# An attention and feed-forward kernel on one core: the turned keys of a unit are written later and read back earlier

## The chip, the cores and the metric

The kernel runs on one core of a Trainium2 chip. The metric is the device time of one execution in microseconds (us). Before the change it is 505.19 us, the median of 3 runs (504.56 to 507.04).

## The reference, cut to what matters

A gated linear attention over 4 batches, 8 heads, 768 steps and a head size of 48 feeds a feed-forward layer with a squared ReLU:

```python
f = 1.0 / (1.0 + np.exp(-f_logit))
for t in range(S):
    state = f[:, :, t, :, None] * state + np.einsum('bhd,bhe->bhde', k[:, :, t], v[:, :, t])
    y[:, :, t] = np.einsum('bhd,bhde->bhe', q[:, :, t], state)
x = y.transpose(0, 2, 1, 3).reshape(B * S, H * D)      # 3072 x 384
h = x @ w_in                                           # 384 -> 2048
r = np.maximum(h, 0.0)
out = (r * r) @ w_out                                  # 2048 -> 384
```

## The kernel before, in words

**Blocks and pieces.** Time is cut into 6 blocks of 128 steps; a block has 512 columns (4 batches by 128 steps). The feed-forward layer of a block goes through 16 pieces of 128 hidden features. For each piece `Moe.run` (L280) issues: `up` (L227, 9 matmuls into a PSUM bank `ph`, two banks taken in turn), `square` (L253, three ACT passes, the last of which writes `gh`), `rest` (L264, one DVE pass that writes `gl` and frees the bank) and `down` (L270, 9 matmuls into the three banks `po`) for the piece two before. Every product is made of three matmuls of high and low parts. The last `down` of a block is owed: it is issued in the first piece of the next block (`before()`, L306), and `finish` (L335) behind it copies the three `po` banks, two on ACT and one on DVE, into tiles `ob` and stores each with a DMA from the SP queue. The tiles `ob` share the buffers of `gh` and `gl` (three of each, L194 and L343), so a later `gh` can only be written when the store that read its buffer has landed. Block 0's second half is an exception: its results are added into tiles `part` of their own.

**Numbering.** After a prologue the pieces run in the order block 1 (pieces 0 to 15), the second half of block 0 (16 to 23), block 2 (24 to 39), block 3 (40 to 55), block 4 (56 to 71), block 5 (72 to 87). Pieces 24, 40, 56 and 72 are first pieces, with the end of the block before in them; so is 16.

**Units.** The attention of a block is 4 units of two heads. Units 8 to 23 (blocks 2 to 5) are woven into the pieces as hooks. The last unit of each block works on keys and queries that the first three hand to it. A unit has a slot, a piece in which its sums are made (`SLOTS`, L65: 12, 14, 18, 20, 22, 28, 31, 34, 37, 44, ...), and for the first three of a block the stages before it stand in `STAGE_AT` (L62), as a number of pieces ahead of the slot and a place in the piece: 0 ahead of `up`, 0.5 behind `square`, 0.7 behind `rest`, 1 at the end of the piece. The stages:
- "L" (L432) and "v" (L441): loads of gates, keys and queries, and of values.
- "GK" (L445, L448) and "Q" (L461): a sigmoid on ACT, then a scan and a product each for keys and queries on DVE, with two small steps on POOL between.
- "t" (`squares`, L514): DVE transposes the keys in squares of 32 by 32 (L517), and four DMAs of SP (L523) write them to `steps` in DRAM, so that time lies along the rows.
- "b" (`back`, L528): one DMA of SP (L530) loads the turned keys from `steps` into `kn`. `kn` has a single buffer.
- The slot itself, at 0.7: "Y" (L594) the outputs of the unit before, "D" (`add`, L545, matmuls L550 of `kn` with the values) and "S" (L556) the sums of this unit, "H" and "X" (L626, L640), which take the outputs of the unit before out of PSUM, then "M", "C" and the moves "m" (L472) and "l" (L532) for the block's last unit.

**What sets the order.** Every engine and the SP queue run their instructions in the order in which the hooks issue them; nothing is reordered. A DMA of SP whose data isn't ready holds all that stand behind it on SP. In one place of one piece, hooks run in the order in which they were registered: the slots and stages unit by unit. Unit 8 has its slot in piece 12 and its "t" in piece 8; unit 9 has its slot in piece 14 and its "t" in piece 10.

Of the kernel before, what the change touches and what calls it, by code (L numbers as in the profile page):

```python
# [58 lines left out]

STAGE_AT = ((-8, 1, "L"), (-5, 0, "v"), (-5, 1, "GK"), (-4, 0.5, "Q"), (-4, 0.7, "t"), (-2, 1, "b"))  # L62
LAST_AT = ((-5, 0, "v"),)

SLOTS = (12, 14, 18, 20, 22, 28, 31, 34, 37, 44, 47, 50, 53, 60, 63, 66, 69)  # L65
# [297 lines left out]
def fast_path(ctx, tc, moe, ident, low, fkqT, vN, w, w4, out):  # L363
# [37 lines left out]
    def weights_load(f, i, mark=False):  # L401
        raw = moe.words(f, i)
        if mark:

            V.memset(raw[0:1, 0:1], 0)
        nc.sync.dma_start(raw, w[f, i].bitcast(I16)[:, 1:])
# [293 lines left out]
    def step(t):  # L700

        nm = t.rstrip("0123456789")
        n = int(t[len(nm) :])  # L710
        if nm == "busy":
            if 0 not in moe.ph:
                moe.bank(0)
            for _ in range(n):
                nc.tensor.matmul(moe.ph[0], lhsT=one.broadcast_to([P, P]), rhs=one.broadcast_to([P, NT]), start=True, stop=True)
        elif nm in ("i", "o"):
            weights_load(n, "io".index(nm))
        elif nm == "j":
            nc.sync.dma_start(moe.fourth_words(), w4.bitcast(I16)[:, 1:])
        elif nm in "enaw":  # L720
            if nm == "e":
                decoding["fourth"] = moe.decode(moe.row4, moe.fourth_parts)
            next(decoding["fourth"])
        elif nm in "AIcJBOdP":
            i = "AIcJBOdP".index(nm) // 4
            if nm in "AB":
                decoding[n, i] = moe.decode(moe.row[n, i], lambda: moe.parts(n, i))
            next(decoding[n, i])
        elif nm in ("ua", "ub", "uc"):
            moe.up_part(n, "abc".index(nm[1]))  # L730
        elif nm == "U" and n < SPLIT:
            moe.up_fourth(n)
        elif nm == "U":
            moe.up(n)
        elif nm == "R":
            moe.square(n)
        elif nm == "E":
            moe.rest(n)
        elif nm == "W":
            moe.down(n)  # L740
        else:
            unit(n).stage(nm)
            if t == "G0":
                for head in moe.head[1:]:
                    nc.scalar.copy(out=head, in_=moe.head[0])
            elif t in ("K1", "K2"):
                for x in xs[0][:2] if n == 1 else xs[0][2:]:
                    G.memset(x[C + 32 :].bitcast(F32), 0.0)
# [7 lines left out]
    with tc.manual_schedule(engines={ET.PE, ET.SP, ET.DVE, ET.Activation, ET.Pool}):  # L756
        with tc.tile_pool(name="ps_p", bufs=2, space=bass.MemoryType.PSUM) as ps_p:
            for t in FIRST.split():
                step(t)
        moe.psum(ctx, "ps_h1", "ps_o")  # L760

        moe.sums_of()
        for t in SECOND.split():
            step(t)
        part = []
        owed = moe.ending(lambda po: part.extend(moe.keep(po)))
        whole = half[0] + half[1]
        order = [(1, whole), (0, half[1])] + [(blk, whole) for blk in range(2, NBLK)]
        hooks = [{} for _ in order]

        def hook(k, n, at, do):
            while n >= len(order[k][1]):
                k, n = k + 1, n - len(order[k][1])
            hooks[k].setdefault((max(n, 0), at), []).append(do)

        def third():
            early.close()
            moe.inputs(ctx)
            xs[2] = moe.new_x(2, 2)

        halves = [(f, i) for f in half[1] for i in range(2)]
        steps = {}

        def advance(h):
            if h not in steps:
                steps[h] = moe.decode(moe.row[halves[h]], lambda: moe.parts(*halves[h]))
            next(steps[h], None)

        for n in range(1, NF - 1):
            few = range(3 * (n - 1) // 2, min(3 * n // 2, len(halves)))
            for h in few:
                if n < AHEAD:
                    weights_load(*halves[h])
                else:
                    hook(0, n - AHEAD, 0.5, lambda h=h: weights_load(*halves[h], mark=True))

            def before(few=few):
                for h, last in zip(few, (None, *few)):  # L800
                    for m in (h, h, last):
                        if m is not None:
                            advance(m)

            def after(few=few[:-1]):
                for h in few:
                    advance(h)

            def last(few=few):
                for h in few[-1:]:  # L810
                    advance(h)
                    advance(h)


            for place, do in zip((0, 0.5, 0.7) if n > 1 else (0.7, 0.7, 0.7), (before, after, last)):
                hook(0, n, place, do)
        hook(0, 12, 0, third)
        later = [Unit(n, xs, (ps_a,)) for n in range(2 * HP, NBLK * HP)]
        for un, last, at in zip((*later, None), (None, *later), SLOTS):
            if un:  # L820
                for n, place, stage in STAGE_AT if un.own else LAST_AT:
                    hook(0, at + n, place, lambda un=un, stage=stage: un.stage(stage))

            def slot(un=un, last=last):
                for who, stage in (last, "Y"), (un, "DS"), (last, "HX"), (un, "rMC"), (un, "ml" * bool(un and un.own)):
                    if who:
                        who.stage(stage)
                if last and not last.own:
                    last.stage("hg")

            hook(0, at, 0.7, slot)
            if un:
                hook(0, at + 1, 0, lambda un=un: un.stage("s"))

        for n in range(2 * NF):
            hook(2 + n // NF, n % NF + SIZES_AT, 1, lambda n=n: moe.sizes(n // 2, n % 2))
        general = []
        found = verdict(nc, moe, low, ident, ps_a)
        for n in range(2):
            hook(len(order) - 2, VERDICT_AT + n, 1, lambda: general.append(next(found)))  # L840
        hook(
            len(order) - 1, VERDICT_AT, 1,
            lambda: general.append(nc.values_load(general[1][0:1, 0:1], min_val=0, max_val=1)),
        )
        for k, (blk, fs) in enumerate(order):
            if blk > 1 and blk + 1 < NBLK:
                xs[blk + 1] = moe.new_x(blk + 1, (0, 1, 2)[blk - 2])
            moe.begin(blk, xs[blk], fs)
            if blk == NBLK - 1:

                moe.third_bank = ps_a
                obs = moe.third_of("ob_last")
                moe.run(hooks[k], obs, owed)
                moe.third_bank = None
            else:
                moe.run(hooks[k], None, owed)
                owed = moe.ending(
                    lambda po, blk=blk: moe.finish(
                        lambda e: out[blk, e * P : (e + 1) * P], None if blk else part, po, blk
                    )  # L860
                )
# [3 lines left out]
def verdict(nc, moe, low, ident, pool):  # L865

    flag = moe.const.tile([1, 1], I32, name="flag")
    good = moe.const.tile([P, 2], F32, name="good")
    nc.vector.tensor_reduce(
        out=good[:, 0:1], in_=low.rearrange("p u n -> p (u n)"), axis=mybir.AxisListType.X, op=ALU.min  # L870
    )
    nc.vector.tensor_scalar(out=moe.sums, in0=moe.sums, scalar1=LARGE, scalar2=None, op0=ALU.is_lt)
    nc.vector.tensor_reduce(out=good[:, 1:2], in_=moe.sums, axis=mybir.AxisListType.X, op=ALU.min)
    nc.vector.tensor_tensor(out=good[:, 0:1], in0=good[:, 0:1], in1=good[:, 1:2], op=ALU.min)
    yield
    pl = pool.tile([1, P], F32, tag="pk", name="pl")
    nc.tensor.transpose(out=pl, in_=good[:, 0:1], identity=ident)
    least = moe.const.tile([1, 1], F32, name="least")
    nc.vector.tensor_reduce(out=least, in_=pl, axis=mybir.AxisListType.X, op=ALU.min)
    nc.vector.tensor_scalar(out=least, in0=least, scalar1=LOWEST, scalar2=None, op0=ALU.is_le)  # L880
    nc.vector.tensor_copy(out=flag, in_=least)
    yield flag
# [185 lines left out]
```

## Time and profile before

| | before |
|---|---|
| median of 3 runs | 505.19 us (504.56 to 507.04) |
| the profiled execution, its own time | 503.3 us |
| its span, first to last instruction | 501.5 us |
| TensorE (PE) busy | 474.3 us, 95% of the span |
| PE weight loads (PEld) | 380.2 us, 76% |
| DVE / ACT / POOL busy | 249.1 / 284.2 / 29.7 us |
| mean granted TensorE clock | 0.987 |

A page of the profile gives busy times by engine, the chain of work that ended last (followed back from the last instruction), the costliest groups of instructions and the DMA issues. The trace behind it can be asked for a timeline of single instructions, for who waited for whom, and for busy times and clock in a stretch. An instruction that waits is not busy; its idle time stands in brackets, with what ended it.

### The profile page before, as it was taken

What the parts mean: (1) busy time and instruction counts of PE and PEld (TensorE: products, weight loads), DVE (VectorE), ACT (ScalarE), POOL (GpSimd) and SP (SyncE); (2) the same over time, 40 slices, a digit from 0 to 9 for tenths busy, and PEclk for the clock granted to TensorE, in tenths of its full rate; (3) what the DMA queues carried; (4) which work ended last, traced back from release to release, by engine and by line L of the source; (5) the groups of instructions that cost most, each with busy time, mean ns of one, the idle gap of its engine ahead of it and who ended that gap; (6) DMA issues with size and microseconds to landing.
All of it is one profiled execution on the core that took longest, in us unless ns stands there. A gap on an engine that the chain in (4) does not pass through costs nothing.

```text
span 501.5 us, 11437 instructions
## 1 busy us (share of the span) xinstructions
PE 474.3 (95%) x4767; PEld 380.2 (76%) x4767; DVE 249.1 (50%) x456; ACT 284.2 (57%) x591; POOL 29.7 (6%) x66
## 2 busy tenths in 40 slices
PE   3889999999599999999999899999899999999995
PEld 2767777887587788878888678888678877888884
DVE  7999853669273646635535443734363232211112
ACT  5599856977255453657565556564654543444441
POOL 5412010000000000000000000000000000000000
PEclk9799999999899999999999999999999999999998
DMA  8887016752707134470333452134431002100001
GB/s 299 247 300 266 14 45 208 241 186 37 169 8 205 27 96 112 126 160 1 86 59 88 119 118 51 31 85 115 119 47 43 3 1 33 66 0 0 1 0 68
DMA packets 64748, 48.65 MB, mean 97 GB/s; under 512 B 46912, under 2 KB 50352, under 8 KB 64688
## 3 DMA queue, kind: packets, MB, share of 16 engines
q1 hardware_dynamic: 64096, 46.78, 33.8%
q0 software_dynamic: 448, 0.92, 0.9%
q8 instruction: 39, 0.64, 0.5%
q14 instruction: 21, 0.17, 0.1%
q10 hardware_dynamic: 144, 0.13, 0.1%
HBM read 35.22 MB, written 7.86 MB: 86 GB/s over the span
## 4 chain that ended last, share of the span: by engine, by line
PE 82%; DVE 6%; DMA 4%; ACT 3%; issue 2%; SPq 2%; POOL 1%; DVEq 0%; POOLq 0%; ACTq 0%
PE po L276 37%; PE ph L249 36%; PE ds L561 2%; PE ds L550 2%; DVE fkq L465 1%; PE py L609 1%; SPq L523 1%; DVE fkq L451 1%; PE ph L609 1%; PE ph L621 1%; DMA raw<-in_w_dram 1%; DMA out_dram<-ob 1%; PE py L621 1%; ACT ph L260 1%; POOL fkq L456 1%
## 5 line engine op out<-in xcount | busy, mean ns | idle before, releaser
L249 PE MATMUL ph<-x,w 128*128 128x512 f32 x864 | 218.4, 398 | 4.7 <-DVE gl L266 3.2
L249 PEld LDWEIGHTS ph<-x,w 128*128 128x128 f32 x864 | 161.4, 188 | 46.0 <-DVE gl L266 4.2
L276 PE MATMUL po<-gh,w 128*128 128x512 f32 x576 | 181.3, 396 | 0.0
L266 DVE TENSOR_TENSOR gl<-ph,gh 128x512 fp32r<-128x512 f32 x96 | 66.3, 690 | 226.9 <-ACT gh L261 226.9
L259 ACT ACTIVATE ph<-ph 128x512 f32<-128x512 f32 x96 | 56.1, 584 | 146.6 <-PE ph L249 146.5
L276 PEld LDWEIGHTS po<-gh,w 128*128 128x128 f32 x576 | 108.6, 188 | 25.2
L276 PE MATMUL po<-gl,w 128*128 128x512 f32 x288 | 116.2, 404 | 0.0
L276 PEld LDWEIGHTS po<-gl,w 128*128 128x128 f32 x288 | 54.3, 189 | 14.1 <-DVE gl L266 0.7
L261 ACT CAST gh<-ph 128x512 fp32r<-128x512 f32 x96 | 56.4, 587 | 9.4 <-DMA out_dram<-ob 6.4
L260 ACT ACTIVATE ph<-ph 128x512 f32<-128x512 f32 x96 | 55.9, 582 | 3.0
L495 ACT COPY sx<-sp 48x208 f32<-48x208 f32 x44 | 16.0, 365 | 25.5 <-DVE sp L583 25.2
L456 POOL TENSOR_SCALAR fkq<-fkq 128x8 f32<-128x8 f32 x18 | 12.3, 685 | 299.6 <-DVE fkq L451 239.4
L451 DVE TENSOR_TENSOR_SCAN fkq<-fz,dr 128x520 f32<-128x520 f32 x18 | 22.2, 1232 | 1.1 <-ACT fz L446 1.1
L465 DVE TENSOR_TENSOR_SCAN fkq<-fz,dz 128x520 f32<-128x520 f32 x18 | 22.3, 1242 | 0.6
L609 PEld LDWEIGHTS py<-sc,vn 64*48 64x48 f32 (+1 forms) x384 | 16.9, 126 | 7.3 <-issue 7.0
L609 PE MATMUL py<-sc,vn 64*48 64x64 f32 (+1 forms) x384 | 21.5, 222 | 0.0
L145 ACT CAST w<-wa 128x384 fp32r<-128x384 f32 (+1 forms) x33 | 16.5, 511 | 6.8 <-DVE wa L136 6.7
L133 ACT CAST head<-raw 128x384 f16<-128x384 bf16 (+1 forms) x33 | 19.6, 627 | 1.1 <-DMA raw<-in_w_dram 1.1
L621 PE MATMUL py<-rx,sx 48*48 48x64 f32 x192 | 19.3, 215 | 0.0
L550 PE MATMUL ds<-vn,kn 64*64 64x48 f32 (+1 forms) x576 | 13.8, 230 | 5.7 <-DMA kn<-steps 5.0
L147 DVE TENSOR_TENSOR w<-wa,w 128x384 fp32r<-128x384 f32 (+1 forms) x33 | 18.0, 548 | 1.3 <-ACT w L145 0.8
L568 DVE TENSOR_TENSOR sc<-ds,mask 128x512 f32<-128x512 f32 x24 | 16.3, 681 | 4.5 <-PE ds L561 4.5
(103 smaller groups left out, 451.9 us busy)
## 6 DMA issues: line engine op xcount, KB each, us to landing
raw<-in_w_dram SPq DMA_DIRECT2D x32, 383.8 KB, 5.7
fkq<-in_fkqT_dram SPq DMA_DIRECT2D x15, 768.0 KB, 5.8
vn<-in_vN_dram SPq DMA_DIRECT2D x24, 192.0 KB, 4.4
steps<-fkq SPq DMA_DIRECT2D x48, 64.0 KB, 2.2
out_dram<-ob SPq DMA_DIRECT2D x12, 256.0 KB, 2.2
kn<-steps SPq DMA_DIRECT2D x12, 224.0 KB, 3.3
fkq<-in_fkqT_dram SPq DMA_DIRECT2D x9, 256.0 KB, 4.5
x<-ys SPq DMA_DIRECT2D x30, 64.0 KB, 2.5
```

What stands on the lines that cost most here:

```text
L133: nc.scalar.copy(out=self.upper(head, F16), in_=high)
L249: self.nc.tensor.matmul(self.ph[f], lhsT=w[:, i], rhs=x[:, j], start=first and n == 0, stop=last and n == 2)
L259: nc.scalar.activation(ph, ph, AF.Relu)
L260: nc.scalar.activation(ph, ph, AF.Square)
L261: nc.scalar.copy(out=gh, in_=ph)
L266: self.nc.vector.tensor_tensor(out=gl, in0=self.ph.pop(f), in1=gh.bitcast(F32), op=ALU.subtract)
L276: self.nc.tensor.matmul(po[e], lhsT=l, rhs=r, start=f == fs[0] and i == 0, stop=f == fs[-1] and i == 2,)
L451: V.tensor_tensor_scan(out=rr[:, ::-1], data0=self.fz[:, NZ * CZ : 0 : -1], data1=dr[:, ::-1], initial=0.0, op0=ALU.mult, op1=ALU.add,)
L465: V.tensor_tensor_scan(out=pp, data0=self.fz[:, : NZ * CZ], data1=dz, initial=0.0, op0=ALU.mult, op1=ALU.add)
L550: nc.tensor.matmul(self.ds[h * C : h * C + m, c, b * D : (b + 1) * D], lhsT=self.kn[rows, b, h * C : h * C + m], rhs=self.vn[rows, b, h * ...
L609: nc.tensor.matmul(self.py[c][h * C : h * C + m, b * C : (b + 1) * C], lhsT=self.vn[rows, b, h * D : h * D + m], rhs=self.sc[rows, h, b], ...
L621: nc.tensor.matmul(self.py[c][h * C : h * C + m, b * C : (b + 1) * C], lhsT=s[rows, b * D : b * D + m], rhs=q[rows], start=False, stop=b = ...
```

## The change

"t" moves from place 0.7 to place 1 of the same piece, four ahead of the slot. "b" leaves the table: it is issued at place 1 three pieces ahead of the slot, instead of two, but not ahead of the slot of the own unit before it, whose sums read the same `kn` buffer. Computation, transfers and their sizes stay as they are.

```diff
-STAGE_AT = ((-8, 1, "L"), (-5, 0, "v"), (-5, 1, "GK"), (-4, 0.5, "Q"), (-4, 0.7, "t"), (-2, 1, "b"))
+STAGE_AT = ((-8, 1, "L"), (-5, 0, "v"), (-5, 1, "GK"), (-4, 0.5, "Q"), (-4, 1, "t"))
...
         later = [Unit(n, xs, (ps_a,)) for n in range(2 * HP, NBLK * HP)]
+        back = 0
         for un, last, at in zip((*later, None), (None, *later), SLOTS):
             if un:
                 for n, place, stage in STAGE_AT if un.own else LAST_AT:
                     hook(0, at + n, place, lambda un=un, stage=stage: un.stage(stage))
+                if un.own:
+
+                    hook(0, max(at - 3, back), 1, lambda un=un: un.stage("b"))
+                    back = at
```

## Rows read from the trace of the kernel before

**Rows 1.** The page: the chain that ended last, shares of the span by engine.

```profile
PE 82%; DVE 6%; DMA 4%; ACT 3%; issue 2%; SPq 2%; POOL 1%; DVEq 0%; POOLq 0%; ACTq 0%
```

**Rows 2.** Waits, whole span: who waited for whom, us in total, times, longest.

```profile
ACT gh L261 <- DMA out_dram<-ob: 6.4, 2, 3.2
...
PE ds L550 <- DMA kn<-steps: 5.0, 1, 5.0
...
PE ph L249 <- DVE gl L266: 3.2, 2, 1.6
```

**Rows 3.** Timeline of SP around slot 12: start, us, instruction.

```profile
115.16 2.67 SPq L523 DMA_DIRECT2D steps<-fkq  x4
...
124.48 2.57 SPq L523 DMA_DIRECT2D steps<-fkq  x4
127.21 0.56 SPq L530 DMA_DIRECT2D kn<-steps  x1
```

**Rows 4.** Timeline of PE in piece 12, in brackets the idle time before.

```profile
123.15 2.27 PE L249 MATMUL ph<-x,w 128*128 128x512 f32 x9
130.45 0.95 PE L550 MATMUL ds<-vn,kn 64*64 64x48 f32 x29 [5.03 <-DMA kn<-steps]
```

**Rows 5.** The chain in order of time, slots 12 and 14: start, us, what.

```profile
135.35 2.11 PE ph L249 x9
...
142.75 0.38 PE ds L550 x24
...
145.98 2.11 PE ph L249 x9
```

**Rows 6.** Stretch behind slot 12: busy of PE, PEld, DVE, ACT, POOL; PEclk, DMA, GB/s.

```profile
131.00:136.00 5.00, 5.00 (x66) 4.20 (x60) 2.02 (x5) 0.73 (x2) 0.00 (x0) 0.72 0.95 242
```

**Rows 7.** The page: DMA issues, count, KB each, median us to landing.

```profile
fkq<-in_fkqT_dram SPq DMA_DIRECT2D x15, 768.0 KB, 5.8
...
steps<-fkq SPq DMA_DIRECT2D x48, 64.0 KB, 2.2
...
kn<-steps SPq DMA_DIRECT2D x12, 224.0 KB, 3.3
```

**Rows 8.** Timeline of ACT: the sigmoid of unit 10 in piece 13.

```profile
139.21 0.63 ACT L446 ACTIVATE fz<-fkq 128x512 f32<-128x512 f32 x1
```

**Rows 9.** Timeline of all engines, pieces 40 and 41.

```profile
274.98 1.10 DVE L517 STREAM_TRANSPOSE fkq<-fkq 128x512 f32<-128x512 f32 x1
...
276.01 0.65 DVE L344 COPY ob<-po 128x512 f32<-128x512 f32 x1
276.11 2.60 SPq L523 DMA_DIRECT2D steps<-fkq  x4
...
278.81 1.54 SPq L345 DMA_DIRECT2D out_dram<-ob  x3
...
281.10 0.59 ACT L261 CAST gh<-ph 128x512 fp32r<-128x512 f32 x1 [3.18 <-DMA out_dram<-ob]
```

**Rows 10.** Timeline, pieces 72 and 73, which have no "t" in them.

```profile
431.30 1.66 SPq L345 DMA_DIRECT2D out_dram<-ob  x3
...
434.40 0.59 ACT L261 CAST gh<-ph 128x512 fp32r<-128x512 f32 x1
```

**Rows 11.** The chain in order of time: pieces 24 and 40 with slots 28 and 44, piece 74.

```profile
194.26 2.11 PE ph L249 x9
...
212.16 0.38 PE ds L550 x23
...
270.38 2.12 PE ph L249 x9
...
290.67 0.35 PE ds L550 x22
...
435.24 2.10 PE po L276 x9
```

**Rows 12.** Waits of the SP queue: us in total, times, longest.

```profile
SPq L530 <- DMA steps<-fkq: 4.9, 6, 1.5
```

## The prediction

> **What bounds the kernel now.** I read the chain of waits by engine first: PE holds 82% of it, DMA 4%, ACT 3%, SP's queue 2% [rows 1]. So TensorE is the bound, and only what makes it stand is worth anything. Next I read who waited for whom [rows 2]. Outside the prologue it shows two things. PE waits once, for 5.0 us, for the load of a unit's turned keys. ACT waits twice, 3.2 us at most, to write `gh` until a store of `ob` has landed, and PE waits twice for `gl`, which comes out of that `gh`. Both holes lie where stages "b" and "t" stand, so I went on with timelines there.
>
> *The hole at slot 12.* PE ends the `up` of piece 12 at 123.15 + 2.27 = 125.42 and starts unit 8's sums only at 130.45, after 5.03 us for `kn` [rows 4]. In SP's queue the four writes of unit 8's "t" left at 115.16, but its "b" left at 127.21 [rows 3]. What stood between is the "t" of unit 9: it is issued in piece 10 at place 0.7, "b" of unit 8 in piece 10 at place 1, so the load waits behind four writes that left from 124.48 to 127.05, after DVE had got to unit 9's transpose. PE pays a second time after the hole: the granted clock from 131 to 136 is 0.72, between the full 2.4 GHz and the half level of 1.2 [rows 6]. From the first sum to the next `up` it takes 135.35 - 130.45 = 4.90 us at slot 12 [rows 4, 5], but 145.98 - 142.75 = 3.23 us at slot 14, at full clock [rows 5]: 1.67 us more.
>
> *The holes at pieces 40 and 56.* In a first piece of a block, "t" at place 0.7 stands ahead of `finish`. On DVE the transpose (1.10 us) runs ahead of the copy of `ob`, and on SP the four writes (2.60 us, from 276.11) run ahead of the stores, which leave at 278.81. ACT was ready for the next `gh` 3.18 us before 281.10, at 277.92, and had to wait until the first store had landed [rows 9]. Piece 56 repeats this; piece 24 has the same hooks, but its `finish` goes to `part`, so nothing there waits for a store. That gives a measure of the loss: from the first `up` of the block to the sums in its fifth piece, 212.16 - 194.26 = 17.90 us in block 2, and 290.67 - 270.38 = 20.29 us in block 3, so 2.39 us lost [rows 11].
>
> **The change part by part.** No instruction, transfer or byte is added or removed; twelve "t" and eleven "b" take other places.
>
> *"b" of unit 8 goes from piece 10 to piece 9*, ahead of unit 9's "t". The writes of unit 8 leave until 115.16 + 2.67 = 117.83 [rows 3]. With 2.2 us to land [rows 7] the load can leave near 120, and with 3.3 us to land it is there at 123.3, 2.1 us before PE asks at 125.42. Gain: 5.03 + 1.67 = 6.70 us.
>
> The wait that goes is a DMA's, so I ask what is late next. Unit 10's load "L" (768 KB) follows unit 9's "t" directly, at about 127.1, and lands after 5.8 us [rows 7], at 132.9. Its sigmoid ran at 139.21 [rows 8]; everything from piece 13 on moves 6.70 us ahead, so it would be due at 132.5. It is 0.4 us late, and DVE's scans, products and the emptying of the outputs' banks in piece 14 hang on it. The cost lies between 0 (slack on DVE takes it) and 0.4; I take 0.2. Unit 9's "b" stays in piece 12 (its predecessor's slot holds it there); its writes have landed by 127.05 + 2.2 = 129.3 and the load by 132.6, while its sums come at 142.75 - 6.7 = 136.0, so it is free.
>
> *"t" to the end of the piece.* Behind `rest` only `finish` and `down` are issued between places 0.7 and 1. `down` is PE's alone, so in most pieces DVE and SP see the same order as before and the move costs and brings nothing. It counts in pieces 24, 40 and 56. In 40, `ob`'s DVE copy (0.65 us) starts at 274.98 where the transpose did [rows 9], and the first store follows ACT's first copy, before that. Piece 72 shows this order undisturbed: stores from 431.30, and the next `gh` at 434.40, 3.10 us later, without a wait [rows 10]. So the wait goes: 2.39 us each at pieces 40 and 56, 4.78 us together. What is late next there is the transpose itself: it ends 0.65 us later, and its writes leave behind three stores (1.54 us), near 277 to 280. Unit 17's sums stand at 290.67 - 2.39 = 288.3 [rows 11]; writes and load need 2.2 + 3.3 us more, so `kn` is there near 285.5. In piece 24 the transpose falls behind three additions, with unit 13's sums ten microseconds off: nothing.
>
> *The other "b", one piece earlier.* Their sums never waited: one wait for `kn` in all is listed [rows 2]. So no gain. The load only needs its writes and the free `kn`; SP waited 4.9 us in 6 of 12 loads for the writes, 1.5 at most [rows 12], with loads behind it that are due pieces later. So the cost is 0 by these rows, and I take that. Above, I bound it by 1.5 us, one such wait paid in full by PE; below nothing is to be had, since no other sum waited.
>
> The rows show "b" waiting on SP itself for its own writes, with its followers behind it [rows 12]. A rule of the Trainium skill bears on that, and speaks against the change: "DMA: Bandwidth & Descriptors", section "Rules for kernel authors", says that a DMA which reads what an earlier DMA wrote has to wait for that one's completion before it is issued. By that rule a reader moved nearer to its writer buys waiting in the queue, which is the third rival below; the trace agrees that the wait is there, but with 1.5 us at most.
>
> **Sum.** 6.70 - 0.2 + 4.78 = 11.3 us. The profiled execution took 503.3 us (span 501.5, 1.8 around it), so it would be 492.0; the median shown is 1.9 above that, and against it I forecast 505.2 - 11.3 = 493.9 us.
>
> **The rivals.**
> 1. *The `gh` wait stays.* The order of `gh` and `ob` buffers could make ACT wait in piece 41 for the owed reads of PE, not for the store. For it: `gh` has three buffers, and the `gh` of the block's first piece is still unread then. Against it: in block 5 `gh` of the second piece starts at 434.40, before the block's first `down` at 435.24 [rows 10, 11]. Only slot 12 gains: 505.2 - 6.5 = 498.7 us.
> 2. *The hole at slot 12 stays in part.* Steps may land late, with `kn` still missing at 125.42, or DVE and ACT, which had the hole to catch up, hold PE in pieces 13 to 15. Against it: 2.1 us of margin. If the clock's 1.67 and half of 5.03 are lost, the time is 493.9 + 4.2 = 498.1 us.
> 3. *Slower: SP becomes the bound.* "b" stands at the head of SP's queue for its writes or for the buffer `kn`, and the store, load or "t" behind it leaves too late, with a hole like that of piece 41 (2.39 us) each time. It decides when the wait exceeds what its followers can spare, and makes the kernel slower than before when that happens at five or more of the eleven units (11.3 / 2.39 = 4.7). With all eleven: 493.9 + 11 × 2.39 = 520.2 us. For it: SP did wait in 6 of 12 [rows 12]. Against it: 1.5 us at most, and the followers are due a piece or more later.
> 4. *The change does nothing:* another DMA's landing and not the order on SP set both waits: 505.2 us. The rows name the queue's order too plainly.
>
> **How the numbers follow.** Forecast 0.82, rival 1 0.07, rival 2 0.07, rival 3 0.02, rival 4 0.02. A measurement of this kernel can tell about 0.5%, 2.5 us, from no change. The first three cases are faster by more than that: 0.96; same 0.02, slower 0.02. The range goes down to 492.3 (the 0.2 not paid, another us from smaller waits that vanish, and the spread of the median) and up to 498.9, so that rivals 1 and 2 lie in it.
>
> **What would show it.** Right: SP issues "b" of unit 8 near 120, between its own writes and unit 9's; PE goes from the `up` of piece 12 to L550 with no wait, and no stretch behind it below full clock; in the first pieces of blocks 3 and 4 the stores leave ahead of the four writes, ACT's wait for the store of `ob` is gone from the waits, and the stretch from first `up` to the fifth piece's sums is 17.9 us in both blocks. Wrong: a wait of L550 for `kn` at any slot, a new wait of ACT or PE behind unit 10's load in pieces 13 to 15, or stores standing behind L530 in SP's queue.

## The result, and the profile after

The changed kernel takes **492.17 us** (median of 4 runs, 492.02 to 492.37) against 505.24 us before (4 runs, 504.56 to 507.04): a ratio of 0.9736, 95% interval 0.9711 to 0.9762. On another chip the same two kernels gave 492.88 and 504.83 us, ratio 0.9763 (0.9744 to 0.9782). The forecast was 493.9 us with a range from 492.3. So the direction and the two holes were right; the time is 1.7 us shorter than forecast and 0.13 us under the range, while the median on the other chip lies inside it. The interest is in those 1.7 us, and in which of the two edits did the work.

| | before | after |
|---|---|---|
| median | 505.24 us | 492.17 us |
| profiled execution, span | 503.3 us, 501.5 us | 492.4 us, 490.7 us |
| PE busy | 474.3 us, 95% | 471.4 us, 96% |
| mean granted clock | 0.987 | 0.999 |

The page after, the chain that ended last by engine. PE has 90% of it where it had 82% [rows 1]:

```profile
PE 90%; DMA 4%; DVE 2%; ACT 1%; SPq 1%; issue 1%; POOL 0%; DVEq 0%
```

**Slot 12.** SP's timeline after the change, to be read against [rows 3]: the load of unit 8's keys (L530) now stands ahead of unit 9's four writes, and left 0.3 us before the "near 120" of the forecast.

```profile
115.35 2.67 SPq L523 DMA_DIRECT2D steps<-fkq  x4
118.06 0.62 SPq L443 DMA_DIRECT2D vn<-in_vN_dram  x1
119.73 0.57 SPq L530 DMA_DIRECT2D kn<-steps  x1
124.68 2.57 SPq L523 DMA_DIRECT2D steps<-fkq  x4
127.35 0.59 SPq L439 DMA_DIRECT2D fkq<-in_fkqT_dram  x1
```

PE's timeline after: the sums start as the `up` of piece 12 ends, with no idle time in brackets [rows 4].

```profile
123.34 2.27 PE L249 MATMUL ph<-x,w 128*128 128x512 f32 x9
125.54 0.60 PE L550 MATMUL ds<-vn,kn 64*64 64x48 f32 x29
...
128.84 2.27 PE L249 MATMUL ph<-x,w 128*128 128x512 f32 x9
```

Busy times and clock in the stretch of [rows 6], after: the clock (the number behind the engines) is 1.00, not 0.72.

```profile
131.00:136.00 5.00, 5.00 (x70) 3.91 (x72) 2.32 (x3) 3.01 (x6) 0.28 (x1) 1.00 1.14 228
```

**First pieces of blocks 3 and 4.** Timeline after, pieces 40 and 41: stores, then transpose, then the four writes. The `gh` of piece 41 starts right behind ACT's second pass, where it waited 3.18 us [rows 9].

```profile
268.78 1.66 SPq L345 DMA_DIRECT2D out_dram<-ob  x3
268.91 0.68 DVE L344 COPY ob<-po 128x512 f32<-128x512 f32 x1
...
269.50 1.08 DVE L517 STREAM_TRANSPOSE fkq<-fkq 128x512 f32<-128x512 f32 x1
...
270.61 2.65 SPq L523 DMA_DIRECT2D steps<-fkq  x4
271.26 0.58 ACT L260 ACTIVATE ph<-ph 128x512 f32<-128x512 f32 x1
271.88 0.59 ACT L261 CAST gh<-ph 128x512 fp32r<-128x512 f32 x1
```

The chain in order of time after: from first `up` to the sums in the fifth piece it is 206.08 - 188.18 = 17.90 us in block 2 and 282.20 - 264.31 = 17.89 us in block 3, which had 20.29 [rows 11].

```profile
188.18 2.11 PE ph L249 x9
...
206.08 0.38 PE ds L550 x23
...
264.31 2.11 PE ph L249 x9
...
282.20 0.38 PE ds L550 x23
```

SP's waits after: all twelve loads now wait for their own writes, 1.6 us at most, where it was 6 of 12 and 1.5 [rows 12]. So the wait that the rule of the Trainium skill ("DMA: Bandwidth & Descriptors", section "Rules for kernel authors") speaks of did come, on SP. It cost PE nothing: outside the prologue PE no longer waits for `kn`.

```profile
SPq L530 <- DMA steps<-fkq: 10.7, 12, 1.6
```

**Where the time went, by stretches.** Between landmarks of PE that all kernels here have (the start of the 18 matmuls of pieces 1 and 2, and the double `down` at the end of each run of pieces), in us:

| trace | to piece 1 | pieces 1 to 15 (slots 12, 14) | 16 to 23 | block 2 | block 3 | block 4 | rest | span |
|---|---|---|---|---|---|---|---|---|
| before | 79.05 | 69.04 | 41.98 | 76.12 | 78.52 | 77.92 | 78.87 | 501.5 |
| after | 79.24 | 62.76 | 41.99 | 76.13 | 76.12 | 75.50 | 78.96 | 490.7 |

The traces give 6.28 us in the stretch with slot 12 and 2.40 + 2.42 = 4.82 us in blocks 3 and 4; the last 0.3 goes the other way at both ends. That is 10.8 us of span, while the medians differ by 13.07. What follows asks two things: which edit closes which hole, and where the kernel before loses some 2 us in its usual executions that its trace doesn't have.

### The profile page after: what moved, and what is told of

Its sections match the earlier page's. It is cut to its first block, busy times and chain, and to the rows that moved or that the text cites. A ratio compares the mean times of both kernels' runs of the same rounds, so it can differ in the third digit from the quotient of the medians.

```text
span 490.7 us, 11434 instructions
## 1 busy us (share of the span) xinstructions
PE 471.4 (96%) x4767; PEld 378.5 (77%) x4767; DVE 249.1 (51%) x456; ACT 284.4 (58%) x591; POOL 29.7 (6%) x66
## 4 chain that ended last, share of the span: by engine, by line
PE 90%; DMA 4%; DVE 2%; ACT 1%; SPq 1%; issue 1%; POOL 0%; DVEq 0%
PE ph L249 41%; PE po L276 41%; DMA raw<-in_w_dram 2%; PE ds L561 2%; PE ds L550 2%; PE py L609 2%; PE ph L609 1%; DMA vn<-in_vN_dram 1%; PE ph L621 1%; PE py L621 1%; SPq L439 1%; DMA x<-ys 1%; DVE fkq L465 1%; DVE gl L266 0%; POOL fkq L456 0%
## 5 line engine op out<-in xcount | busy, mean ns | idle before, releaser
L136 DVE SCALAR_TENSOR_TENSOR wa<-raw,head 128x384 int32<-128x384 int32 (+1 forms) x33 | 17.4, 545 | 1.5 <-ACT head L133 1.5
L159 ACT ACTIVATE junk<-w 128x384 f32<-128x384 f32 x32 | 16.8, 526 | 0.1
```

## The experiments

### Which edit does it

**Only the loads move** ("b" as in the change, "t" at 0.7; the diff is against the changed kernel).

```diff
-STAGE_AT = ((-8, 1, "L"), (-5, 0, "v"), (-5, 1, "GK"), (-4, 0.5, "Q"), (-4, 1, "t"))
+STAGE_AT = ((-8, 1, "L"), (-5, 0, "v"), (-5, 1, "GK"), (-4, 0.5, "Q"), (-4, 0.7, "t"))
```

> Only the loads "b" move (as in the change), "t" stays at place 0.7. Both theories: no wait for kn at slot 12, the waits of ACT for the store of ob at pieces 41 and 57 stay as before (3.2 us each), the stretch from piece 40's up to slot 44's sums stays 20.3 us. In the traces the changed kernel is only 10.8 us shorter than before, though the medians differ by 13.1; what is open is where the kernel before loses some 2 us more, and scatters by 2.5 us, in the executions that are not the profiled one. Theory A (it is the hole at slot 12, whose cost in clock differs between executions): this kernel comes to 503.3 - 6.4 = 496.9 us and its runs agree within 0.5 us. Theory B (it is the holes at pieces 41 and 57): 505.2 - 6.4 = 498.8 us, and its runs still scatter by 1 us or more.

Measured: 499.04 us (497.48 to 499.71). The hole at slot 12 is gone and those of blocks 3 and 4 stay. Waits, whole span:

```profile
ACT gh L261 <- DMA out_dram<-ob: 6.8, 2, 3.6
...
PE ph L249 <- DVE gl L266: 3.6, 2, 2.0
```

The runs lie 2.2 us apart, as theory B has it; but in this trace the extra is ahead of piece 1 (81.03 us, against 79.05 before the change), which neither theory said.

**Only "t" moves** ("b" two ahead, as before).

```diff
-STAGE_AT = ((-8, 1, "L"), (-5, 0, "v"), (-5, 1, "GK"), (-4, 0.5, "Q"), (-4, 0.7, "t"), (-2, 1, "b"))
+STAGE_AT = ((-8, 1, "L"), (-5, 0, "v"), (-5, 1, "GK"), (-4, 0.5, "Q"), (-4, 1, "t"), (-2, 1, "b"))
```

> Only "t" moves to the end of its piece, "b" stays two ahead. Both theories: the stores of ob leave ahead of the four writes, the two waits of ACT are gone, the stretches of blocks 3 and 4 from first up to the fifth piece's sums are 17.9 us. The hole at slot 12 stays. Now unit 9's "t" and unit 8's "b" stand at the same place of piece 10, in the order in which they were registered, so "b" of unit 8 goes ahead of unit 9's "t" and leaves SP before 124. Then the hole at slot 12 would go with "t" alone, and the time is that of the whole change, 492.2 us. If the order is the other way round, Theory A: 505.2 - 4.8 = 500.4 us with a scatter above 1 us; Theory B: 503.3 - 4.8 = 498.5 us, scatter below 0.5 us.

Measured: 492.36 us (492.02 to 492.95), the whole change. Both holes are gone. SP's timeline shows why slot 12 closes though "b" keeps its place: at place 1 of piece 10 unit 8's load was registered before unit 9's "t", so it goes first.

```profile
119.69 0.57 SPq L530 DMA_DIRECT2D kn<-steps  x1
124.64 2.75 SPq L523 DMA_DIRECT2D steps<-fkq  x4
```

**Only unit 8's load moves**, one piece earlier.

```diff
-                    hook(0, at + n, place, lambda un=un, stage=stage: un.stage(stage))
+                    hook(0, at + n - (stage == "b" and at == SLOTS[0]), place, lambda un=un, stage=stage: un.stage(stage))
```

> Only unit 8's "b" moves, from piece 10 to piece 9; all other stages as before. My account: the same as with all eleven loads moved, within 0.5 us, since no other load was waited for (496.9 us by theory A, 498.8 by theory B). Rival: the other ten loads are worth something of their own, then this kernel is more than 0.5 us slower than the one with all of them moved.

Measured: 497.78 us (497.25 to 498.24), not slower than with all loads moved, so the ten others bring nothing. From piece 1 to block 4 its stretches agree with those of all loads moved within 0.05 us; its 80.01 us ahead of piece 1 against 81.03 make 1.0 of the 1.3 us between the medians.

**Only loads move, again**, for that difference.

> The kernel with only the loads moved, again. Its median was 1.3 us above that of the kernel with only unit 8's load moved, though the stretches of the two traces agree within 0.05 us from piece 1 on and the whole difference lies ahead of piece 1 (81.0 against 80.0). If that was chance in the prologue (theory C), the median now falls to 498.3 us or less, and the stretch ahead of piece 1 in the trace differs from 81.0 while the others stay. If the ten other loads cost something with "t" at place 0.7, it stays at 499 us.

Measured: 497.01 us (496.69 to 498.20), with 79.42 us ahead of piece 1. So the 499 did not come back, as theory C has it, and the stretches from piece 1 to block 3 agree with the first trace within 0.03 us. The extra lay ahead of piece 1, where no edit here changes an instruction. The two runs were on different chips; whether it was chance or the chip they don't tell.

**Only SP's order in the first pieces**: the transpose stays ahead of `finish`, and its four DMAs become a stage "u" of their own behind it.

```diff
-STAGE_AT = ((-8, 1, "L"), (-5, 0, "v"), (-5, 1, "GK"), (-4, 0.5, "Q"), (-4, 0.7, "t"), (-2, 1, "b"))
+STAGE_AT = ((-8, 1, "L"), (-5, 0, "v"), (-5, 1, "GK"), (-4, 0.5, "Q"), (-4, 0.7, "t"), (-4, 1, "u"), (-2, 1, "b"))
...
```

> The transpose of "t" stays at place 0.7 and only its four DMAs go to place 1; "b" stays two ahead. My account: what counts is the order on SP alone, the first store of ob hangs on ACT's copy and not on DVE's, so the waits of ACT for the store are gone as in the changed kernel, and unit 8's load is ahead of unit 9's writes again: 492.3 us, like the kernel with only "t" moved, with 17.9 us from the first up to the sums of the fifth piece in blocks 3 and 4. Rival: DVE's order counts too (the copy of ob behind the transpose holds the second store, and so a gl or gh buffer): 1 us or more at each of pieces 40 and 56, 494.3 us or more.

Measured: 492.24 us (492.07 to 492.83), block 3 at 76.13 and block 4 at 75.48 us. DVE's order doesn't count: in the timeline the transpose still runs ahead of DVE's copy, the first store leaves with ACT's copy, and `gh` of piece 41 doesn't wait. So at these pieces the order on SP alone does the work.

```profile
268.87 1.08 ACT L344 COPY ob<-po 128x512 f32<-128x512 f32 x2
...
269.49 2.65 SPq L345 DMA_DIRECT2D out_dram<-ob  x3
269.62 1.10 DVE L517 STREAM_TRANSPOSE fkq<-fkq 128x512 f32<-128x512 f32 x1
...
270.64 0.65 DVE L344 COPY ob<-po 128x512 f32<-128x512 f32 x1
...
272.59 0.59 ACT L261 CAST gh<-ph 128x512 fp32r<-128x512 f32 x1
```

### What the hole at slot 12 costs

**The hole filled with matmuls**: the kernel before, PE busy while it waits.

```diff
+FILL = 22
...
+                if at == SLOTS[0]:
+                    for _ in range(FILL):
+                        nc.tensor.matmul(moe.spare(), lhsT=one.broadcast_to([P, P]), rhs=one.broadcast_to([P, NT]), start=True, stop=True)
```

> The kernel before with 22 matmuls of nothing (128 columns of ones by 512, into a bank that the next up overwrites) put on PE in front of unit 8's sums at slot 12; nothing else moves. The wait for kn stays, but PE is busy in most of it, some 4.7 of 5.0 us. If the clock pays 1.67 us behind the hole, and more in other executions (theory A): the sums and the next up take 3.3 us in place of 4.9, time 501.6 us, and runs within 0.5 us of each other. If the clock has no part in it: 503.3 in the profiled run, and the scatter stays. Theory B: 505.2 - 1.7 = 503.5 us with the scatter left.

Measured: 501.94 us (501.29 to 503.06), ratio 0.9944 (0.9925 to 0.9964): **2.9 us** less than before in the medians, with the wait as long as it was: the sums start at 130.56, 5.03 us behind the end of `up`. Timeline of PE, and the stretch behind, where the clock is now 1.00 and was 0.72 [rows 6]:

```profile
125.66 4.97 PE L828 MATMUL ph<-one 128*128 128x512 bf16 x22
```

```profile
131.00:136.00 5.00, 5.00 (x66) 4.11 (x57) 2.02 (x5) 0.73 (x2) 0.00 (x0) 1.00 1.01 250
```

In its trace pieces 1 to 15 take 67.59 us, 1.45 less than in the first trace before. So the fill gives twice as much in the medians as against that one trace. The runs still lie 1.8 us apart, so the clock behind this hole isn't all of the scatter.

**Two more traces of the kernel before.**

> The kernel before, unchanged, for a second trace of it: the profiled execution had a span of 501.5 us, but twelve other executions had 501.0 to 504.9, 503.1 in the middle, while the changed kernel has 490.2 to 490.7 in all. The stretches are measured between PE's landmarks: the start to piece 1's up (79.1 us in the first trace), from there to the end of block 0 (111.0), block 2 (76.1), block 3 (78.5), block 4 (77.9), the rest (78.9). Theory A: what a longer execution has more lies in the stretch with slot 12 (above 111.0), where the clock is down behind the hole for a time that differs. Theory B: it lies in blocks 3 and 4 (above 78.5 and 77.9). Theory C: it lies ahead of piece 1, in the prologue, which the change does not touch (above 79.1; the trace of the kernel with only the loads moved has 81.0 there, at a lower clock).

> The same as the run before it: a third trace of the kernel before. Theories A, B and C as there; what they say has to hold in this trace too, and the sum of the stretches' differences to the first trace has to be the difference of the spans.

Measured: spans of 502.3 and 501.1 us; pieces 1 to 15 take 70.09 and 69.24 us, ahead of piece 1 it is 79.40 and 78.95, and blocks 2 to 4 agree with the first trace within 0.1. So theory B falls. Of the second trace against the first, A holds for 1.05 us and C for 0.35, and the rest of the kernel gives 0.6 back, which makes the 0.8 us between the spans. The hole is the same, the clock behind it differs. Timeline of PE and busy times of two stretches, second trace:

```profile
130.74 0.95 PE L550 MATMUL ds<-vn,kn 64*64 64x48 f32 x29 [4.98 <-DMA kn<-steps]
```

```profile
131.00:136.00 5.00, 5.00 (x72) 4.21 (x66) 2.02 (x5) 0.73 (x2) 0.00 (x0) 0.50 0.99 248
126.00:138.00 12.00, 7.26 (x79) 6.07 (x80) 3.09 (x7) 3.08 (x7) 0.00 (x0) 0.72 0.80 176
```

The longer stretch, from 126 to 138 us, holds all the time that the clock was down in the wait and behind it. In the first trace it has 0.86, in the second and third 0.72. First trace:

```profile
126.00:138.00 12.00, 7.55 (x86) 6.37 (x87) 2.74 (x7) 3.24 (x8) 0.00 (x0) 0.86 0.75 173
```

**The hole put back into the changed kernel**, beside the changed kernel on one chip.

```diff
-                    hook(0, max(at - 3, back), 1, lambda un=un: un.stage("b"))
+                    if at == SLOTS[1]:
+                        hook(0, 10, 1, lambda: later[0].stage("b"))
+                    if at > SLOTS[0]:
+                        hook(0, max(at - 3, back), 1, lambda un=un: un.stage("b"))
```

> The changed kernel with the hole at slot 12 put back: unit 8's "b" stands in piece 10 behind unit 9's "t" again, everything else as changed, so pieces 40 and 56 stay closed. It prices that hole by medians. In the first trace of the kernel before it costs 6.3 us, in the second, with the clock at the half level through all of 131 to 136, 1.05 us more. Theory A (the clock's part differs and the first trace was one of the cheap ones): 492.2 + 5.0 + 2.9 = 500.1 us, the 2.9 being what filling the hole with matmuls gave in the medians, and runs 1 us or more apart. Rival (1.67 us for the clock, and the rest from elsewhere): 498.5 us.

> The changed kernel again, on the chip on which the others of this call run: 492.2 us, runs within 0.5 us. The others of the call are compared with it.

Measured: 500.69 us (498.88 to 502.10) and 492.88 us (492.10 to 494.74). The hole costs **7.81 us** in the medians. The kernel's runs form two groups, spans of 497.2, 497.3 and 497.8 and of 500.1, 500.3 and 500.3 us; the trace is of the short one (69.37 us for pieces 1 to 15, 6.6 more than without the hole). The median is the mean of 499.51 and 501.88, one run of each group, and no run lies near it; by the short group alone the hole costs 6.2 us, by the long one 9.1. The changed kernel's own runs were wider apart than expected; its trace has 81.59 us ahead of piece 1, 2.3 more than the first one, and the same stretches from there to block 4 within 0.1.

With the loads-only kernel on the same chip the prices add up: 7.81 us for slot 12, 497.01 - 492.88 = 4.13 us for blocks 3 and 4, together 11.94; the kernel before is 504.83 - 492.88 = 11.95 us above. With runs that scatter by 1.5 to 3.2 us, so close a match is luck.

**Four traces to catch the long group.**

> The kernel with the hole at slot 12 put back fell into two groups, spans of 497.2 to 497.8 and of 500.1 to 500.3 us; its trace is of the first group (69.4 us from piece 1 to the end of block 1's pieces, up of piece 13 at 5.1 us behind the first sum). Four more traces of it, to catch one of the second group. Theory A: in that one the hole itself is as long as here (5.0 us), the granted clock behind it stays at the half level longer, and the stretch is 72 us or more, all other stretches and the prologue the same. Theory C: the stretch stays 69 to 70 us and the 2.9 us lie ahead of piece 1.

The other three had the same expectation. Measured: spans of 497.9, 497.3, 497.0 and 498.0 us, with 69.52, 69.34, 69.28 and 70.07 us for pieces 1 to 15 and 79.6, 79.0, 79.1 and 79.6 ahead. None is of the long group, so these runs don't decide. The clock from 126 to 138 us is 0.72 in all four, as in the second and third trace before. What differs is when it falls, so from the first sum to the next `up` they take 5.03 to 5.82 us.

**The hole put back and filled**, beside it unfilled.

> The changed kernel with the hole at slot 12 put back, and 22 matmuls of nothing on PE in that hole. The hole's wait is the same, only PE is busy in it. If the clock behind the hole makes the group of executions near 500 us span (theory A), that group is gone: all spans at 495.7 to 496.9, time 497.5 to 498.5 us, 2 us or more below the kernel with the hole unfilled beside it. If the long group stays at spans near 500, its cause is not the clock behind this hole.

> The changed kernel with the hole at slot 12 put back, unfilled, beside the filled one on one chip: again two groups of spans, about 497 to 498 and about 500, median 499 to 500.7 us.

Measured: filled 497.58 us (496.98 to 498.30), unfilled 500.00 us (498.83 to 501.21). All spans of the filled one lie between 495.3 and 496.6, those of the unfilled one between 497.1 and 499.5; two clear groups did not return. Keeping PE busy in an unchanged wait is worth 2.42 us in the medians, and no run of the filled kernel is as long as the shortest of the other. What made the spans of 500.1 to 500.3 us on the other chip these runs can't show, since they have no such group to take away.

### A version that goes further

In the changed kernel PE's longest wait behind the prologue is one for DVE at piece 19. It stood in the kernel before too (0.77 us), and the prediction's list of waits left it out. Its timeline after the change:

```profile
160.28 0.97 PE L249 MATMUL ph<-x,w 128*128 128x512 f32 x3 [0.76 <-DVE x L643]
```

Unit 12's "Q" stands ahead of `gl` of piece 18 and of the outputs of unit 9 (L643) there. Here "Q" goes to the end of piece 18; the diff is against the changed kernel.

```diff
+                    if at == SLOTS[4] and stage == "Q":
+                        place = 1
```

> The changed kernel with one thing more: the stage "Q" of the unit with slot 22 goes from the middle of piece 18 to its end, behind slot 18 (its own "t" follows it there). In the changed kernel PE waits there for DVE: gl of piece 18 and the outputs of unit 9 stand behind Q's scan and product, and up of piece 19 starts 160.28 - 158.95 = 1.3 us later than its matmuls would allow. My account: that 1.3 us goes, 490.9 us. Rival: the scan only moves in front of the transpose and of gl of piece 19, which then holds up piece 20: no gain, 492.2 us.

> The changed kernel with unit 12's "Q" behind slot 18, again, beside the changed kernel on one chip: the trace gave 1.07 us less in the stretch with piece 18, so 491.1 us if that is all; rival, no gain beyond 0.3 us.

Measured: 491.53 us (490.83 to 491.79) beside 492.24 us of the kernel with SP's order alone; and 492.18 us (490.90 to 492.59) beside 492.88 us of the changed kernel. Pieces 16 to 23 take 40.92 us, not 41.99, in both traces. The stretch is 1.07 us shorter, of 1.3 expected; the medians say 0.7, and runs of the two kernels overlap, since the prologue scatters by more.

## Why the prediction was right or wrong

**Which work bounds, and the two holes: right.** Both are gone, PE's clock stays up, and the stretches of the traces agree: 4.82 us in blocks 3 and 4 for the forecast 4.78, and 6.28 us at slot 12 for 6.70 - 0.2. Of the rivals, ACT's wait is gone, so `gh` waited for the store (rival 1); `kn` was there in time, and only DVE's part of rival 2 came, with 0.28 us (below); SP waited in front of every "b", and PE paid nothing for it (rival 3); the order on SP set both waits (rival 4).

**Where it failed: the term "1.67 us more" for the clock behind the hole, and the sum built on it.** I took it from one execution, and read it too large there: the row at 142.75 in [rows 5] is where the chain joins slot 14's sums, not their start. By the timeline alone it is 135.19 - 130.45 = 4.74 us at slot 12 [rows 4] and 145.82 - 142.54 = 3.28 us at slot 14, so 1.46 us more, and the filled kernel's trace says 1.45.

```profile
135.19 2.27 PE L249 MATMUL ph<-x,w 128*128 128x512 f32 x9
...
142.54 0.58 PE L550 MATMUL ds<-vn,kn 64*48 64x48 f32 x29
...
145.82 2.27 PE L249 MATMUL ph<-x,w 128*128 128x512 f32 x9
```

This slip made the forecast gain too large. The size failed the other way: of the nine traces with the hole unfilled, that execution paid the least. The other eight took 5.00 to 5.85 us from the first sum to the next `up`, at a clock of 0.72 from 126 to 138 us, not 0.86. The runs that fill the hole put the clock's part at 2.9 and 2.4 us in the medians, and the hole put back costs 7.81 us, where my two terms, with the 0.2 that I took off, made 6.5. By the fill, 2.9 - 1.45 = 1.5 of the 1.9 us by which the profiled 503.3 lay under the median are accounted for; for the rest the prologue's scatter is the only other place that the traces show. The step "the median shown is 1.9 above that, and against it I forecast 505.2 - 11.3" carried the whole 1.9 over to the changed kernel as if it were a constant of the measurement. By these prices most of it belonged to the hole, and went with it: 503.3 - 11.3 = 492.0 us would have been 0.2 off. The range had the same fault: its lower end allowed for "the spread of the median", not for a term that is small in one execution and larger in others. That the median fell under the range by 0.13 us, and not just inside it, is chance: the two chips differ by 0.7.

By medians of one chip the forecast 11.3 was 11.95: 1.3 more at slot 12, 0.65 less in blocks 3 and 4, where the traces have 4.82. Both are within the scatter of the runs. The first comparison gave 13.07; the intervals of the two ratios overlap, and the runs don't tell what of the 1.1 us between them is the chips and what the prologue.

**Also wrong: which edit closes slot 12.** I gave it to the load's earlier piece and wrote of "t" that it "counts in pieces 24, 40 and 56". It counts in piece 10 as well: at place 1 it falls behind unit 8's load, which stood at place 1 already. With "t" alone the time is 492.36 us; the moved loads add nothing to that, and alone they close only slot 12. Two hooks at one place of one piece have an order too, by registration, and I hadn't looked it up for the changed table.

**The small terms.** Unit 10's load, the 0.2, came, and with it a sign that I had named for being wrong, a new wait of ACT in piece 13. SP issued the load at 127.35; it took 6.3 us to land, and the sigmoid, which had not waited before [rows 8], waited 0.71 us. DVE's scans, and then its passes over the outputs of unit 8 (L643), came later, and the weight load of `up` of piece 15 waited for those. Timelines of ACT, PEld and PE after the change:

```profile
133.67 0.63 ACT L446 ACTIVATE fz<-fkq 128x512 f32<-128x512 f32 x1 [0.71 <-DMA fkq<-in_fkqT_dram]
139.63 1.94 PEld L249 LDWEIGHTS ph<-x,w 128*128 128x128 f32 x9 [0.44 <-DVE x L643]
139.63 2.38 PE L249 MATMUL ph<-x,w 128*128 128x512 f32 x9
```

That `up` follows the one of piece 13 by 139.63 - 128.84 = 10.79 us, before by 145.82 - 135.19 = 10.63, and to `up` of piece 16 it is 17.21 us for 16.93: 0.28 us lost (0.16 to 0.41 in the nine traces with slot 12 closed). So the mechanism was right and the size near. The other "b", taken at 0, cost 0.

**Left open.** What made the long executions of the kernel with the hole put back isn't shown: no trace has one. Over such an execution the mean granted clock was 0.983 to 0.986, over a short one 0.992 or 0.993, but such a mean doesn't say where the clock was down; and on the same chip the changed kernel without the hole had spans from 490.4 to 493.0 us, with the extra of its trace ahead of piece 1. So the prologue stays a rival of the clock behind the hole. Why the prologue takes 79.0 to 81.6 us in executions of unchanged instructions is open too. The loads-only kernel had a clock of 0.55 from 20 to 30 us in its 81.03 us trace and 1.00 in its 79.42 us trace, but the kernel before had 0.77 there and 79.05 us, the changed kernel's second trace 0.81 and 81.59 us.

## What to carry to other kernels

In a queue that keeps its order, look at the pairs: a load that somebody waits for behind writes that nobody waits for is a hole, and swapping two hooks closes it without a byte less. Where the profiled execution lies under the median, ask which stretch varies before the difference is treated as a constant; if it is the stretch that the change removes, it goes too. Take both ends of a stretch from one view and from the same instruction. Price a hole's clock by keeping the engine busy in it, over several runs, not by one trace.

## What the runs showed of the hardware

Behind an equal wait of PE (4.96 to 5.03 us) the granted clock from 126 to 138 us was 0.86 of full in one trace and 0.72 in eight, and from 131 to 136 us it was between 0.50 and 0.72: part of the time at the level of 1.2 GHz, not 2.4. From the first sum to the next `up` PE then took 4.74 to 5.85 us, and 3.30 in the two traces with 22 matmuls in the wait, where the clock stayed at 1.00; those runs were 2.4 and 2.9 us faster in the medians. Twelve DMAs that stood in SP's queue until their own data had landed (10.7 us in all) cost PE nothing.
